# The middle steps' second product on GpSimd in four groups of six, and its two additions joined into one

## Chip, cores and metric

The kernel runs on one core of one Trainium2 chip. The metric is the device time of one execution in microseconds (us). Five engines work side by side: TensorE (PE in the profile, with its weight loads as PEld), VectorE (DVE), ScalarE (ACT), GpSimd (POOL) and SyncE (SP), which here only issues DMAs.

## What is computed

Two blocks follow each other, all in float32. The first mixes a sequence in the frequency domain: a real FFT over 3008 tokens, a product with a complex filter, and the inverse FFT, for 8 images with 256 channels. The second is a gated feed-forward block over the 24064 resulting tokens.

```python
X = np.fft.rfft(x, axis=1)                    # x: 8 x 3008 x 256
y = np.fft.irfft(X * (filt_r + 1j * filt_i)[None], n=3008, axis=1)
x = y.reshape(8 * 3008, 256)
g = x @ w_gate                                # 256 x 1536
silu = g * (1.0 / (1.0 + np.exp(-g)))
out = (silu * (x @ w_val)) @ w_out            # 1536 x 256
```

## The kernel before

**Tiling.** The FFT is done as small matrix products, in three stages: along one factor of the length, then with the twiddle factors and the filter (the middle steps), then back. The feed-forward block takes an image in 4 chunks (k), and each chunk in 3 groups (g) of the hidden width, so an image has 12 groups, numbered 0 to 11 (`step = 3 * k + g` from the second image on). A group multiplies sums of activations by sums of weights (tokens P, Q, A, B, E with their pairs), which saves products at the price of additions: those fall to VectorE, ScalarE and GpSimd.

**The order of the work** is written out by hand. `SCHEDULE` (line 87) is one list of tokens for a whole group; a loop over it (line 1384) issues each token's instructions, and every engine works through its own in that order (`pin`, which keeps program order). A token with a quote mark belongs to the group before. Tokens that matter here:

- `P Q A B E`: products on TensorE (line 1036), into banks `wk`, `wa`, `we`
- `x s y e`: what is put into a bank before a product is added to it; `e13` is such an operation on VectorE (line 333, output `we`), `y` the same into SBUF
- `m l g u h v`: copies and activations on ScalarE (lines 1071, 1078), subtractions and products on VectorE (lines 329, 1083)
- `D`: differences on GpSimd (line 329, `D<-f,f`); `S`: the sums of products that the output projection needs, on GpSimd too (lines 326 and 329, `h<-h`); `S00'` and `S01'` come first, near the start of the next group
- `n1 n2 n3`: the next chunk's sums (`combine_sequence`, GpSimd and ScalarE, output `y_t`). They are issued only where the group is the last of its chunk (`sequence_of`, line 1287), that is in groups 2, 5, 8 and 11
- `W`, `o`, `z`, `x.o`: output projection, its additions on VectorE, a transposition on VectorE, and the output DMAs on SP's queue
- `b0` to `b7`: one more piece of the next image's FFT at each of them (line 1399)

**The middle steps.** While images 1 to 6 are in the feed-forward block, the next image is prepared in these pieces. `fours(w)` (line 739) is one middle step, a generator that stops at each `yield` and goes on at the next `b` token; w = 0 to 6 runs in groups 4 to 10 (line 1346). For w below 6 it does, in turn: the products of the first stage's values (line 761, bank `wqb`); copies of these to SBUF on ScalarE (`raw`, line 775); the product with the real part of the filter on VectorE (line 779, into y); at `b4` the DMAs that bring `raw`, with real and imaginary rows swapped, into a tile q (line 596, `lent<-raw`); at `b5` and `b6` the product of q with the other part of the filter, half of the tile each (line 818); at `b7` the additions y = y + q on GpSimd (line 326, `lent<-lent`, 128x512), and the DMA that loads the next step's filter (`load_filter`, line 727, `lent<-filter`) into the same buffer. The next step's products read y at its `b0` (line 749).

x, y, q, filter and the tables of these steps all lie in one SBUF tile, `lent`, by which name the profile knows them. Reloads of the group's weights (`wt_t<-w_all`, line 477) go through SP's queue as well, at the tokens Q2, A12, A23 and B03, each when the matmuls that read the old weights are done.

Of the kernel before, what the change touches and what calls it, by code (L numbers as in the profile page):

```python
# [44 lines left out]
ALU = mybir.AluOpType  # L45
# [158 lines left out]
def kernel(  # L204
# [10 lines left out]
    nc = tc.nc  # L215
# [43 lines left out]
    def room_of(tag, u=0):  # L259

        first, units, count = fours[tag]
        a = (first + u % count * units) * NV * C
        return lent[:, a:a + units * NV * C]
# [31 lines left out]
    pin = tc.keep_in_program_order  # L295
# [29 lines left out]
    def add(eng, dst, a, b):  # L325
        return eng.tensor_tensor(out=dst, in0=a, in1=b, op=ALU.add)  # L326

    def sub(eng, dst, a, b):
        return eng.tensor_tensor(out=dst, in0=a, in1=b, op=ALU.subtract)  # L329
# [239 lines left out]
    def bank(name):  # L569
        return wps.tile([128, 512], FP32, name=f"w{name}", tag="w")  # L570
# [10 lines left out]
    class Spectral:  # L581
# [157 lines left out]
        def fours(self, w):  # L739

            tb = self.tb.pop(w)
            home, there = [], []
            if w:
                home = [bank(f"qc_{self.b}_{w}_{e}") for e in range(2)]
                y = self.p.pop(w - 1)
                for s in (0, 2, 1, 3):
                    for e in range(2):
                        r = slice(64 * e, 64 * e + 64)
                        pin(nc.tensor.matmul(  # L749
                            out=home[e][s // 2 * 64:s // 2 * 64 + 64, s % 2 * C:s % 2 * C + C],  # L750
                            lhsT=tb[r, 1, 64 * s:64 * s + 64], rhs=y[r, s],
                            start=s % 2 == 0, stop=True, skip_group_check=True))
            if w < N_FOUR:
                t = self.t2.pop(w)
                there = [bank(f"qb_{self.b}_{w}_{p}") for p in range(2)]
                for s in range(2):
                    for e in range(2):
                        for p in range(2):
                            r = slice(64 * p, 64 * p + 64)
                            a = 64 * (2 * s + e)  # L760
                            pin(nc.tensor.matmul(  # L761
                                out=there[p][64 * e:64 * e + 64, ts(s, C)],
                                lhsT=tb[r, 0, a:a + 64], rhs=t[r, s, e],
                                start=s == 0, stop=True, skip_group_check=True))
            yield
            z = y = None
            raw = []
            if w < N_FOUR:
                y = self.p[w] = room_of("y").rearrange("p (s c) -> p s c", c=C)
                there = [t.rearrange("p (s c) -> p s c", c=C) for t in there]  # L770

            def keep(p):
                t = t1pool.tile([128, NV, C], FP32, name=f"raw_{self.b}_{w}_{p}", tag="t1", bufs=2)
                raw.append(t)
                pin(nc.scalar.copy(out=t, in_=there[p]))

            def real(p):
                a = slice(2 * p, 2 * p + 2)
                pin(nc.vector.tensor_tensor(out=y[:, a], in0=there[p], in1=self.f[w][:, 0, a],
                                            op=ALU.mult))  # L780

            if home:
                z = room_of("g").rearrange("p (h f) -> p h f", h=2)
                pin(nc.scalar.copy(out=z[:, 0], in_=home[0]))
                pin(sub(nc.vector, z[:, 1], z[:, 0], home[1]))
            if there:
                keep(0)
            yield
            if home:
                pin(add(nc.vector, z[:, 0], z[:, 0], home[1]))  # L790
            if there:
                keep(1)
                real(0)
            yield
            if there:
                real(1)
            if home:
                rows = self.d2_tokens.rearrange("(h n) (r s) c -> (n r) h (s c)", h=2, r=2)
                for p in range(2):
                    at = (4 * w - 4 + 2 * p) * C  # L800
                    pin(nc.scalar.dma_start(out=rows[:, :, at:at + 2 * C],
                                            in_=z[64 * p:64 * p + 64]))
            yield
            q = None
            if there:
                q = room_of("e").rearrange("p (s c) -> p s c", c=C)
                for p in range(2):
                    pairs = [t.rearrange("(q r) s c -> q r s c", r=2)
                             for t in (q[:, 2 * p:2 * p + 2], raw[p])]
                    for r in range(2):  # L810
                        self.load(out=pairs[0][:, r], in_=pairs[1][:, 1 - r])
                self.load_four(w + 1)
            self.load_turns(w + 1)
            yield
            for half in range(2):
                a = slice(2 * half, 2 * half + 2)
                if there:
                    pin(nc.vector.tensor_tensor(out=q[:, a], in0=q[:, a], in1=self.f[w][:, 1, a],  # L818
                                                op=ALU.mult))
                yield  # L820
            for half in range(2 if there else 0):
                a = slice(2 * half, 2 * half + 2)
                pin(add(nc.gpsimd, y[:, a], y[:, a], q[:, a]))
            if there:
                self.f.pop(w)
            self.load_filter(w + 1)

# [503 lines left out]
    for b in range(B):  # L1331
# [35 lines left out]
        for step in range(NCHUNK * NG + (b == B - 1)):  # L1367
# [16 lines left out]
            for place, token in enumerate(SCHEDULE):  # L1384
# [4 lines left out]
                op = token.rstrip("'")  # L1389
# [76 lines left out]
```

## Time and profile before

| | us |
|---|---|
| three timed runs | 2838.08, 2839.66, 2836.62 |
| median | 2838.08 |
| the profiled run | 2833.91 |
| its span, first to last instruction | 2832.1 |

| what | count | mean ns | busy us |
|---|---|---|---|
| line 818, VectorE, 128x512 (the second product) | 72 | 959 | 69.1 |
| line 779, VectorE, 128x512 (the first product) | 72 | 682 | 49.1 |
| line 326, GpSimd, `lent<-lent` 128x512 | 84 | 1271 | 106.8 |
| line 326, GpSimd, `h<-h` 128x376 | 190 | 986 | 183.4 |
| line 329, GpSimd, `h<-h` 128x376 | 572 | 999 | 558.7 |
| line 333, VectorE, `we<-wk,c` 128x376 | 96 | 547 | 52.6 |
| line 1036, TensorE, 188 columns, `wa` | 4464 | 323 | 879.2 |

72 of the 84 in the third row are the additions of the middle steps; the other 12 belong to the second image's preparation. The granted clock of TensorE is 0.998 of its full speed, and one group lasts about 28.5 us.

How such rows are read: a group's row gives its line, engine and operation, what it writes and reads by the program's names, the shape, how often it ran, the busy time and the mean. A timeline's row starts with the start in us from the span's beginning and the duration; "x4" says how many instructions are merged; in brackets stands how long the engine was idle before, and what ended that. Matmuls overlap, and a duration of 0.80 for four of them is longer than their spacing.

### The profile page before, as it was taken

The page shows a single profiled execution, that of the slowest core. Times are in us where ns is not written, and L with a number is a line of the kernel's source. Part 1 is how long each engine was busy: PE and PEld are TensorE (multiplying, and loading weights), DVE is VectorE, ACT ScalarE, POOL GpSimd, SP SyncE. Part 2 cuts the span into 40 slices and gives each one's busy share as a digit, 9 for nine tenths or more (in the row PEclk, how much of TensorE's full clock was granted, in tenths as well). Part 3 has the DMA queues.
Part 4 walks back from the last instruction along what each step waited for, and adds up shares of the span by engine and source line. Part 5 has one row for each costly group of instructions (what it writes and reads, how often), then busy time and mean ns, then how long its engine had stood idle before and what let it go on. Part 6 is the DMA issues. An engine that isn't in the chain of part 4 may idle for free.

```text
span 2832.1 us, 48560 instructions
## 1 busy us (share of the span) xinstructions
PE 2784.2 (98%) x15432; PEld 2312.1 (82%) x15432; DVE 2033.8 (72%) x4603; ACT 1565.8 (55%) x4202; POOL 1524.9 (54%) x1671
## 2 busy tenths in 40 slices
PE   7999999999999999999999999999999999999998
PEld 5777878888888888788888888888888888888887
DVE  6898766777667767677766677667776767766666
ACT  6775445555555555555555555555554555555554
POOL 4886576464545554446554455444555454545543
PEclk9999999999999999999999999999999999999999
DMA  9687866877666775767666676667766777655543
GB/s 231 216 274 251 270 209 217 291 234 229 180 187 205 246 225 168 204 217 226 218 183 201 213 240 201 186 191 234 227 203 179 215 222 224 194 147 153 152 137 82
DMA packets 363373, 586.59 MB, mean 207 GB/s; under 512 B 198388, under 2 KB 246260, under 8 KB 363024
## 3 DMA queue, kind: packets, MB, share of 16 engines
q1 hardware_dynamic: 337922, 534.73, 60.8%
q10 hardware_dynamic: 23406, 45.43, 5.9%
q0 software_dynamic: 1792, 3.34, 0.5%
q8 instruction: 125, 2.05, 0.3%
q14 instruction: 128, 1.05, 0.1%
HBM read 467.87 MB, written 101.34 MB: 201 GB/s over the span
## 4 chain that ended last, share of the span: by engine, by line
PE 85%; DVE 4%; POOL 3%; issue 2%; DMA 1%; ACT 0%; SPq 0%; POOLq 0%; DVEq 0%
PE wa L1036 23%; PE wk L1036 16%; PE wA L1133 16%; PE we L1036 12%; PE wG L1133 8%; PE wF L1133 4%; PE pd L939 3%; PE wqa L690 2%; PE wqc L749 1%; PE wqb L761 1%; POOL out_dram L1118 1%; POOL h L329 1%; DVE lent L818 1%; DVE y L333 1%; DVE o L326 0%
## 5 line engine op out<-in xcount | busy, mean ns | idle before, releaser
L1036 PE MATMUL wa<-y_t,wt_t 128*128 128x188 f32 x4464 | 879.2, 323 | 6.8 <-DMA y_t<-yt 2.0
L1036 PEld LDWEIGHTS wa<-y_t,wt_t 128*128 128x128 f32 x4464 | 745.6, 190 | 84.8 <-ACT wa L1062 11.1
L1036 PEld LDWEIGHTS wk<-y,wt_t 128*128 128x128 f32 x2976 | 494.7, 190 | 106.1 <-issue 33.4
L1036 PE MATMUL wk<-y,wt_t 128*128 128x188 f32 x2976 | 571.2, 325 | 0.0
L329 POOL TENSOR_TENSOR h<-h 128x376 f32<-128x376 f32 x572 | 558.7, 999 | 15.4 <-DVE h L326 15.2
L326 POOL TENSOR_TENSOR h<-h 128x376 f32<-128x376 f32 x190 | 183.4, 986 | 702.5 <-DVE h L1083 702.5
L1133 PE MATMUL wA<-h,wo_t 128*128 128x376 f32 x1532 | 551.1, 482 | 3.6 <-DVE o L326 3.5
L1036 PE MATMUL we<-y_t,wt_t 128*128 128x188 f32 x2232 | 433.6, 323 | 5.1 <-DVE we L333 4.2
L329 POOL TENSOR_TENSOR D<-f,f 128x376 f32<-128x376 f32 x288 | 279.6, 985 | 253.9 <-ACT f L1051 253.8
L329 DVE TENSOR_TENSOR we<-we,m 128x376 f32<-128x376 f32 x576 | 318.5, 554 | 120.0 <-PE we L1036 62.4
L1036 PEld LDWEIGHTS we<-y_t,wt_t 128*128 128x128 f32 x2232 | 368.2, 190 | 10.4 <-DVE we L333 8.2
L1133 PEld LDWEIGHTS wA<-h,wo_t 128*128 128x128 f32 x1532 | 274.9, 190 | 113.7 <-issue 10.7
L1071 ACT COPY m<-wa 128x376 f32<-128x376 f32 x576 | 273.0, 474 | 86.7 <-PE wa L1036 83.4
L333 DVE SCALAR_TENSOR_TENSOR y<-wk,c 128x376 f32<-128x376 f32 x480 | 246.4, 539 | 57.7 <-ACT c L1055 35.3
L1078 ACT ACTIVATE g<-wa 128x188 f32<-128x188 f32 x576 | 187.8, 326 | 163.9 <-PE wa L1036 153.3
L1078 ACT ACTIVATE u<-we 128x188 f32<-128x188 f32 x576 | 188.5, 328 | 155.3 <-DVE we L329 148.9
L1133 PE MATMUL wG<-h,wo_t 128*128 128x376 f32 x768 | 274.0, 479 | 0.0
L1055 ACT COPY c<-wk 128x376 f32<-128x376 f32 x288 | 136.3, 473 | 221.2 <-PE wk L1036 194.2
L1051 ACT ACTIVATE f<-wk 128x376 f32<-128x376 f32 x288 | 140.4, 487 | 169.3 <-PE wk L1036 133.1
L1067 ACT COPY we<-y 128x376 f32<-128x376 f32 x480 | 221.8, 481 | 18.8 <-DVE h L1083 14.5
L1083 DVE TENSOR_TENSOR h<-wa,g 128x188 f32<-128x188 f32 x576 | 198.4, 345 | 33.0 <-ACT g L1078 32.8
L1083 DVE TENSOR_TENSOR h<-we,u 128x188 f32<-128x188 f32 x576 | 197.4, 343 | 27.0 <-ACT u L1078 16.0
(162 smaller groups left out, 3512.9 us busy)
## 6 DMA issues: line engine op xcount, KB each, us to landing
wt_t<-w_all SPq DMA_DIRECT2D x174, 896.0 KB, 4.8
wt_t<-w_all SPq DMA_DIRECT2D x174, 768.0 KB, 4.5
lent<-filter SPq DMA_DIRECT2D x36, 1024.0 KB, 6.9
lent<-d SPq DMA_DIRECT2D x84, 256.0 KB, 4.6
d<-lent ACTq DMA_DIRECT2D x84, 256.0 KB, 3.8
d<-lent ACTq DMA_DIRECT2D x96, 192.0 KB, 3.3
lent<-raw SPq DMA_DIRECT2D x144, 128.0 KB, 2.8
t<-d SPq DMA_DIRECT2D x112, 128.0 KB, 4.5
```

Source lines behind the costliest of these rows:

```text
L326: return eng.tensor_tensor(out=dst, in0=a, in1=b, op=ALU.add)
L329: return eng.tensor_tensor(out=dst, in0=a, in1=b, op=ALU.subtract)
L333: return nc.vector.scalar_tensor_tensor(out=dst, in0=a, scalar=-1.0, in1=b, op0=ALU.mult, op1=ALU.subtract)
L939: pin(nc.tensor.matmul(out=rows, lhsT=self.t4[k, i][:, j, ts(cb, 128)], rhs=cols, start=j == 0, stop=True, skip_group_check=True))
L1036: pin(nc.tensor.matmul(out=ps[:, z], lhsT=self.wt[:, SLOT[p], z], rhs=rhs, start=start and z == 0, stop=True, skip_group_check=True))
L1051: pin(act.mul(self.small(f"f{i}", f"f{i}", 1), t[f"k{i}"], -1.0))
L1055: pin(act.copy(out=self.small(f"c{i}", f"c{i}", 1), in_=t[f"k{i}"]))
L1067: pin(act.copy(out=self.bank(f"e{at}"), in_=t[f"y{at}"]))
L1071: pin(act.copy(out=self.small(f"m{at}", "m", 4), in_=t[f"a{at}"]))
L1078: pin(act.activation(out=self.small(op, "g", 3, 1)[:, 0], in_=ps[:, 1], func=AF.Silu))
L1083: pin(v.tensor_tensor(out=dst, in0=ps[:, 0], in1=g, op=ALU.mult))
L1133: pin(nc.tensor.matmul(out=self.tiles[at], lhsT=wo_t[:, JB * q + i, WO[p], :], rhs=self.hs[i][:, HID[p]], start=start and i == 0, stop=Tru ...
```

## The change

In the middle steps, the second product of w = 0, 2, 3 and 5 is issued on GpSimd; w = 1 and 4 stay on VectorE. For all w the two additions of half a tile become one of the whole tile (128x1024), issued once both halves of the product are made. The tokens at which all of these are issued stay the same.

```diff
             for half in range(2):
                 a = slice(2 * half, 2 * half + 2)
                 if there:
-                    pin(nc.vector.tensor_tensor(out=q[:, a], in0=q[:, a], in1=self.f[w][:, 1, a],
-                                                op=ALU.mult))
+                    e = nc.vector if w % 3 == 1 else nc.gpsimd
+                    pin(e.tensor_tensor(out=q[:, a], in0=q[:, a], in1=self.f[w][:, 1, a],
+                                        op=ALU.mult))
                 yield
-            for half in range(2 if there else 0):
-                a = slice(2 * half, 2 * half + 2)
-                pin(add(nc.gpsimd, y[:, a], y[:, a], q[:, a]))
             if there:
+                pin(add(nc.gpsimd, y, y, q))
                 self.f.pop(w)
             self.load_filter(w + 1)
```

## Prediction

> **What bounds the kernel now.** I began with the page's table of engines:
>
> ```profile
> PE 2784.2 (98%) x15432; PEld 2312.1 (82%) x15432; DVE 2033.8 (72%) x4603; ACT 1565.8 (55%) x4202; POOL 1524.9 (54%) x1671
> ```
>
> TensorE is busy for 98% of the span, so an edit on VectorE or GpSimd can only win back moments in which TensorE stands still. The second view is the list of waits, for TensorE alone, between 560 and 2450 us, where all the middle steps lie. It has one line:
>
> ```profile
> PE we L1036 <- DVE we L333: 4.2, 12, 0.3
> ```
>
> Twelve waits, always for the operation of line 333 that fills a bank `we` before products are added to it. Six images are prepared in this stretch, so that is two waits an image. To place them I went to the timeline of one group with such a wait (627 to 645 us, image 2's preparation, w = 2), first on VectorE and TensorE:
>
> ```profile
> 636.33 0.34 DVE L1083 TENSOR_TENSOR h<-wk,g 128x188 f32<-128x188 f32 x1
> 636.59 1.07 DVE L818 TENSOR_TENSOR lent<-lent 128x512 f32<-128x512 f32 x1
> 637.58 0.34 DVE L1083 TENSOR_TENSOR h<-wa,g 128x188 f32<-128x188 f32 x1
> 637.85 0.53 DVE L333 SCALAR_TENSOR_TENSOR y<-wk,c 128x376 f32<-128x376 f32 x1
> 638.30 1.31 DVE L818 TENSOR_TENSOR lent<-lent 128x512 f32<-128x512 f32 x1
> 639.53 0.54 DVE L333 SCALAR_TENSOR_TENSOR y<-wk,c 128x376 f32<-128x376 f32 x1
> ...
> 641.06 0.53 DVE L329 TENSOR_TENSOR we<-we,m 128x376 f32<-128x376 f32 x1
> 641.49 0.55 DVE L333 SCALAR_TENSOR_TENSOR we<-wk,c 128x376 f32<-128x376 f32 x1
> ...
> 640.93 0.82 PE L1036 MATMUL wa<-y_t,wt_t 128*128 128x188 f32 x4
> 642.09 0.90 PE L1036 MATMUL we<-y_t,wt_t 128*128 128x188 f32 x4 [0.34 <-DVE we L333]
> ```
>
> Read: VectorE runs without a break from 636.33 to 642; the two operations of line 818 are in that row; the product E13 (the `we` at 642.09) waits for e13 (the line 333 at 641.49). Such a block of four matmuls normally follows the last one after 0.64 us (the two `wa` blocks at 582.26 and 582.90 us, for example). Here it came after 1.16: 0.52 us lost. The view of waits counts 0.34 because it subtracts a modelled end. Measured start to start over all matmuls of the stretch, the twelve losses sum to 6.1 us, and w = 1 of the last prepared image (2321.25 us) loses another 0.23. The other gaps there are shorter than 0.12 us and stand at the same places in groups that have no line 818.
>
> **Why line 818 is dear in those groups.** It lasts 0.68 us in some places and 1.07 or 1.31 in others. The difference is GpSimd:
>
> ```profile
> 635.15 1.96 POOL L329 TENSOR_TENSOR h<-h 128x376 f32<-128x376 f32 x2
> 637.79 1.27 POOL L326 TENSOR_TENSOR lent<-lent 128x512 f32<-128x512 f32 x1 [0.68 <-PE wa L1036]
> 639.74 1.27 POOL L326 TENSOR_TENSOR lent<-lent 128x512 f32<-128x512 f32 x1 [0.68 <-DVE lent L818]
> ```
>
> The first half at 636.59 overlaps the subtraction that ends at 637.11, the second at 638.30 overlaps the addition of the first half. Of the 72, the 36 that touch no GpSimd operation average 0.680 us, the 36 that do 1.238.
>
> **What the Trainium skill says.** (1) "GPSIMD Engine Reference", section Key points: GpSimd shares its SBUF interfaces with VectorE, and VectorE instructions with two SBUF inputs contend. The trace agrees exactly: line 818 is the only VectorE group of the stretch whose two inputs both lie in SBUF, and the only one that lengthens. y of line 333 (one input in PSUM) takes 0.538 us under GpSimd and 0.539 clear of it, h of line 1083 0.346 and 0.345. (2) The same page, section Elementwise — side-by-side cycle accounting, gives 4497 ns on GpSimd against 2293 on VectorE for a two-input addition, and puts it down to the reading of two operands, not the arithmetic. The trace agrees in size: 1.271 us (addition, 128x512) against 0.680 is 1.87 times.
>
> **The change, part by part.** The steps of w = 0 to 5 fall into groups 4 to 9 of an image; w % 3 = 1 are groups 5 and 8, the last of a chunk, where GpSimd also forms the next sums. So w = 0, 2, 3, 5 move: 4 x 6 images x 2 halves = 48 of 72 multiplications.
>
> *VectorE* loses 48 slots. For w = 2 and 5 the slot is 0.99 + 1.23 us (636.59 to 637.58, 638.30 to 639.53), so 2.2 us in front of e13. What else could hold e13? It stands behind l12 (line 329), whose matmul E12 begins at 639.02 and is read from 639.82 on. Then e13 starts at about 640.25 and ends at 640.8; E13's regular place is 640.93 + 0.64 = 641.57. Margin 0.77 us: the 0.51 vanishes whole. Gain 6.1 us. For w = 0 and 3 the slots are 4 x 0.60 us an image, but no matmul waits in those groups: worth nothing.
>
> *GpSimd* gains 48 multiplications, which no row shows. Lower bound: a read of 512 elements at VectorE's speed, 0.68; upper: twice the addition, 2.5, since the arithmetic isn't what the page names as the limit. I take the addition's 1.27. From the rows of 376, 512 and 564 elements (0.985, 1.271, 1.383) an element costs 2.1 ns, so one addition of 1024 is an estimated 2.36 us instead of 2 x 1.27. Per group: 2 x 1.27 + 2.36 = 4.9 us. In w = 2 GpSimd comes free at 637.11 and ends at 642.0 (with 2.5: 644.5); its next work, the first sum of products of the group's S step, starts at 649.54, when VectorE's h is ready. 7.5 us are left (5.1). The result is read by the next group's products, later still. Cost nothing, hidden by GpSimd's idle time at each group's end (702.5 us in the row of that subtraction's idle time). The swapped halves arrive 3.2 us after their DMA issue (last issue of w = 2 at 628.0), before GpSimd comes free; where they come later (w = 3: 662.4 + 3.2 = 665.6, GpSimd free at 663.6) nothing stands behind the wait.
>
> *Slowing others.* The moved operations contend only with VectorE's two-SBUF-input ones, of which none is left in these groups. 0.
>
> *SP.* The next filter's load may start once the second multiplication has read the buffer: for w = 2 639.61 so far, now 637.11 + 2.54 = 639.65. Next in SP's queue is a reload of weights at 643.66, waiting for TensorE. 0 at 1.27, and 0 up to 3.0 us a multiplication.
>
> *w = 1 and 4* keep VectorE, but the joined addition now waits for both halves, so the second half no longer overlaps the first addition: 1.31 becomes 0.68, and with it goes the stray 0.23 (there the half lasted 1.60). GpSimd's addition ends at 610.91 + 2.36 = 613.3 instead of 612.9, and the sums behind it (612.90, 0.98 us, then 1.57 idle until ScalarE) shift by 0.4 within that idle time: 0. Fewer additions, 72 to 36: 0 off the path.
>
> *Sum:* -6.1 - 0.23 = -6.3 us on a span of 2832.1, hence 2825.8. That profiled run took 2833.91 us; the three timed ones 2836.62 to 2839.66. Applied to their median: 2838.08 - 6.3 = **2831.7**. Timed runs could have more strays of w = 1 and 4: twelve times 0.23 would be 2.8 more, 2829.
>
> **Rivals.**
> *A. As summed*, 2831.7, own range 2828.5 to 2833.
> *B. Part of the stall comes back.* E13 is released, and a ScalarE copy in the same row becomes the next limit. For: ScalarE's g at 640.10 sat 2.26 us behind y. Against: that y itself is delayed by line 818 and moves ahead with it; s23, the next one that a matmul needs, has about 0.8 us by the same count. Half the gain: 2835.
> *C. Nothing comes of it*, because e13 was held by l12's inputs and not by VectorE's row. Against: w = 0, 1 and 3 run the same tokens with no stall. 2838.
> *D. Slower: the multiplication on GpSimd is far dearer than its addition.* Place: w = 2 and 5, ahead of the next group's S step. GpSimd has 649.54 - 637.11 = 12.4 us for 2m + 2.36, so it decides from m = 5.0 us; beyond, each us of m delays twelve groups by 2 us. At m = 5.6: 12 x 1.2 = 14 us, less 6.3: 2846. For: no row shows m. Against: four times the addition.
> That the change does not do what it says is excluded by the group numbers above.
>
> **How the numbers follow.** A 0.66, B 0.14, C 0.12, D 0.08. A measurement can tell about 0.2% (5.7 us, 2832.4) from no change. A is faster by 0.22%, just beyond it, and I count 0.06 of it as falling within; B and C are within; D is slower. Range: down to A's strays, up to no change, which leaves out D and half of C above and little below: 2828.5 to 2838.1.
>
> **What would show it.** Right: no TensorE wait for line 333 in 560 to 2450 us; GpSimd multiplications near 1.27 us; joined additions near 2.36; the remaining 24 on VectorE all at 0.68. Wrong: GpSimd's first S subtraction of a group begins late after VectorE's h; a new wait of TensorE on ScalarE behind E13; SP's weight reload issued late.

## The result, and the profile after

The change makes the kernel faster by more than was predicted: 2827.52 us against 2837.22 for the kernel before, medians of six runs each; the ratio is 0.9965, with a 95% interval from 0.9953 to 0.9978. Forecast were 2831.7, and at least 2828.5. The profiled run of the changed kernel has a span of 2824.2 us.

The page's table of engines, after:

```profile
PE 2781.0 (98%) x15432; PEld 2314.5 (82%) x15432; DVE 1991.2 (71%) x4555; ACT 1572.9 (56%) x4202; POOL 1577.9 (56%) x1683
```

VectorE lost 42.6 us of busy time and GpSimd gained 53; neither figure says what the span does. The groups of instructions, with shapes kept apart, show what was built (busy us, mean ns; then idle time before):

```profile
L326 POOL TENSOR_TENSOR lent<-lent 128x1024 f32<-128x1024 f32 x36 | 85.0, 2362 | 42.1 <-PE wA L1132 40.2
L819 POOL TENSOR_TENSOR lent<-lent 128x512 f32<-128x512 f32 x48 | 60.4, 1283 | 1.2 <-PE pd L938 1.1
...
L819 DVE TENSOR_TENSOR lent<-lent 128x512 f32<-128x512 f32 x24 | 16.4, 682 | 0.0
```

The multiplication costs on GpSimd what the addition did, the joined addition costs 2.36 us, and the 24 that stay on VectorE are all at 0.68. The list of TensorE's waits between 560 and 2450 us, which had the one line for `we`, is empty. The timeline at the same place of the schedule as before (w = 2, image 2's preparation), VectorE first, then GpSimd and TensorE:

```profile
637.03 0.34 DVE L1082 TENSOR_TENSOR h<-wk,g 128x188 f32<-128x188 f32 x1
637.29 0.34 DVE L1082 TENSOR_TENSOR h<-wa,g 128x188 f32<-128x188 f32 x1
637.55 1.00 DVE L333 SCALAR_TENSOR_TENSOR y<-wk,c 128x376 f32<-128x376 f32 x2
639.28 0.55 DVE L326 TENSOR_TENSOR o<-o,wA 128x376 f32<-128x376 f32 x1 [0.73 <-PE wA L1132]
...
641.09 0.55 DVE L333 SCALAR_TENSOR_TENSOR we<-wk,c 128x376 f32<-128x376 f32 x1
...
637.76 2.52 POOL L819 TENSOR_TENSOR lent<-lent 128x512 f32<-128x512 f32 x2
640.36 2.37 POOL L326 TENSOR_TENSOR lent<-lent 128x1024 f32<-128x1024 f32 x1
649.61 1.92 POOL L326 TENSOR_TENSOR h<-h 128x376 f32<-128x376 f32 x2 [6.88 <-DVE h L1082]
...
641.62 0.80 PE L1035 MATMUL wa<-y_t,wt_t 128*128 128x188 f32 x4
642.26 0.80 PE L1035 MATMUL we<-y_t,wt_t 128*128 128x188 f32 x4
```

VectorE now has pauses, E13 follows its predecessor after the regular 0.64 us, and GpSimd still waits 6.88 us for the next group's first sum.

**Where the time came from.** The trace gives the start of every matmul. From the first matmul of W2 in a group to that of the next is one group's length. For one undisturbed image (image 2), in us, with the groups that the change shortened:

| kernel | w = 1 | w = 2 | w = 3 | w = 4 | w = 5 | whole image |
|---|---|---|---|---|---|---|
| before | 27.685 | 28.279 | 30.842 | 27.687 | 28.287 | 341.46 |
| after | 27.609 | 27.612 | 30.816 | 27.612 | 27.610 | 339.93 |
| gain | 0.08 | 0.67 | 0.03 | 0.08 | 0.68 | 1.53 |

w = 0 and 6, and the five other groups, are equal to 0.01 us. Over the images that prepare another one (1 to 6) the lengths fall from 2045.05 to 2036.05 us, 9.0; one of these images has an unrelated 0.21 in the changed kernel, without which it is about 9.2.

The spans differ by only 7.9. The rest stands where no edited line runs: image 0 takes 377.2 us in the first profile of the kernel before and 378.7 after, while the head and the tail of the span together are 0.4 shorter after. A second look at the kernel before (last experiment) gives 379.7 for image 0. So the first profile was a short draw, and the timed difference of 9.7 us belongs beside the 9.2, not beside 7.9; the interval of the ratio reaches from 6 to 13 us.

### The profile page after: what moved, and what is told of

It is laid out like the page before. It is cut to its first block, busy times and chain, and to the rows that moved or that the text cites. A ratio compares the mean times of both kernels' runs of the same rounds, so it can differ in the third digit from the quotient of the medians.

```text
span 2824.2 us, 48474 instructions
## 1 busy us (share of the span) xinstructions
PE 2781.0 (98%) x15432; PEld 2314.5 (82%) x15432; DVE 1991.2 (71%) x4555; ACT 1572.9 (56%) x4202; POOL 1577.9 (56%) x1683
## 3 DMA queue, kind: packets, MB, share of 16 engines
q14 instruction: 128, 1.05, 0.1%
## 4 chain that ended last, share of the span: by engine, by line
PE 82%; POOL 1%; issue 1%; DVE 0%; DMA 0%; ACT 0%; POOLq 0%; ACTq 0%; DVEq 0%
PE wa L1035 22%; PE wk L1035 15%; PE wA L1132 15%; PE we L1035 11%; PE wG L1132 7%; PE wF L1132 4%; PE pd L938 3%; PE wqa L690 1%; PE wqc L749 1%; PE wqb L761 1%; POOL out_dram L1117 0%; POOL h L329 0%; DMA out_dram<-o 0%; DVE o L326 0%; DVE h L329 0%
```

## Experiments

The diffs are against the changed kernel, unless they say otherwise. Each result's interval is that of the ratio to the kernel before, measured in the same series. Lengths of an image are read from W2 to W2 as above, on images 2 to 5, leaving out those in which a group without an edited line is 0.1 to 0.5 us longer in that run alone.

### Joined additions alone

```diff
-                    e = nc.vector if w % 3 == 1 else nc.gpsimd
+                    e = nc.vector
```

> All multiplications stay on VectorE; only the two additions become one. Theory 1 (contention): E13 is late because the halves of line 818 are stretched by GpSimd; without an addition between the halves the second one takes 0.68 us instead of 1.31, e13 comes 0.6 us sooner, and the stall in w = 2 and 5 is gone (regular groups of 27.6 us, an image 339.9 to 340.2 us from step to step against 341.43 before). Gain 7.5 to 9 us, as large as that of the whole change. Theory 2 (occupancy): any line 818 on VectorE in those groups is too much; w = 2 and 5 keep a stall of at least 0.3 us, an image stays at 340.7 or more, and the gain is below 5 us.

Measured: 2827.47 us against 2836.52, ratio 0.9968 [0.9956, 0.9980]; an image 339.94 to 339.97 us, w = 2 at 27.63. This is the whole gain, with not one operation moved to GpSimd. All instructions of line 819 in this kernel (min/median/max in ns), and then w = 2's timeline on VectorE and GpSimd:

```profile
L819 DVE TENSOR_TENSOR lent<-lent x72: 674/680/1093, 582.6 to 2428.0; 128x512 f32<-128x512 f32 x72
```

```profile
639.98 1.09 DVE L819 TENSOR_TENSOR lent<-lent 128x512 f32<-128x512 f32 x1
640.99 0.34 DVE L1082 TENSOR_TENSOR h<-wa,g 128x188 f32<-128x188 f32 x1
641.26 0.53 DVE L333 SCALAR_TENSOR_TENSOR y<-wk,c 128x376 f32<-128x376 f32 x1
641.71 0.68 DVE L819 TENSOR_TENSOR lent<-lent 128x512 f32<-128x512 f32 x1
...
638.56 1.96 POOL L329 TENSOR_TENSOR h<-h 128x376 f32<-128x376 f32 x2
642.52 2.37 POOL L326 TENSOR_TENSOR lent<-lent 128x1024 f32<-128x1024 f32 x1 [2.00 <-PE wA L1132]
```

The first half still meets the subtraction that ends at 640.52 and takes 1.09. The second has GpSimd to itself and takes 0.68, where it took 1.31. These 0.63 us are enough: e13 comes in time, and TensorE has no wait for line 333 between 560 and 2450 us. Theory 2 falls.

### Moved multiplications alone

```diff
             if there:
-                pin(add(nc.gpsimd, y, y, q))
+                for half in range(2):
+                    a = slice(2 * half, 2 * half + 2)
+                    pin(add(nc.gpsimd, y[:, a], y[:, a], q[:, a]))
                 self.f.pop(w)
```

> Multiplications of w = 0, 2, 3, 5 on GpSimd, the additions still two. Both theories: the stall in w = 2 and 5 is gone with its 0.10 us of restart (12 x 0.62 = 7.4 us), since no line 818 is left on VectorE there. w = 1 and 4 keep the second half stretched to 1.31 us and with it 0.05 us of stall each, and the 0.02 us ahead of W1 in five groups stays if it comes from the second addition's wait: an image of 340.1 to 340.2 us against 339.94 of the change. Gain 7 to 8 us.

Measured: 2829.53 us, ratio 0.9977 [0.9968, 0.9986]; an image 340.14 to 340.16 us, w = 1 and 4 at 27.68, w = 2 and 5 at 27.63. As expected in each part: the stall is gone this way too, the 0.05 us of w = 1 and 4 stay, and so do 0.024 us ahead of W1 in five groups an image. The timed difference to the joined additions alone is 2 us, and the two intervals overlap; the 0.2 us an image is read from the traces.

### All multiplications on GpSimd

```diff
-                    e = nc.vector if w % 3 == 1 else nc.gpsimd
+                    e = nc.gpsimd
```

> All multiplications on GpSimd, w = 1 and 4 too, additions joined. If GpSimd has room there (its row was idle for 2.0 and 0.7 us before the two additions, and the multiplications can start when its S work ends, at about 607.7 us of 612.9), w = 1 and 4 stay at 27.61 us and an image at 339.9: the same as the change within 1 us. If the sums behind are pushed back, the first sums of products (S00) come late in the groups after them, W1 waits for them, and the groups after w = 1 and 4 lengthen by up to 1 us each: up to 12 us slower than the change.

Measured: 2825.47 us, ratio 0.9969 [0.9956, 0.9981]; an image 339.93 us, w = 1 and 4 at 27.61. GpSimd has the room, and keeping w = 1 and 4 off it wasn't needed. In time the two kernels can't be told apart.

### The changed kernel again

> The changed kernel once more, beside the other three on the same chip, so that they can be set against it: 9 to 10 us below the kernel before, an image of 339.94 us in the trace.

Measured: 2828.10 us, ratio 0.9973 [0.9962, 0.9984]; an image 339.93 us.

### The overlap put back

Against the joined additions alone:

```diff
             if there:
+                pin(add(nc.gpsimd, raw[0], y[:, 0:2], q[:, 0:2]))
                 pin(add(nc.gpsimd, y, y, q))
```

> As the kernel with joined additions alone (all multiplications on VectorE), plus one addition on GpSimd of the first half of y and q into a tile that nobody reads: it waits for the first multiplication only, as the old first addition did, so GpSimd works again beside the second half of line 818. Extra work in all 36 middle steps; the output is unchanged. Contention: the second half goes back to 1.31 us in w = 1, 2, 4 and 5, the stall of 0.51 us with its restart of 0.1 returns in w = 2 and 5, and 0.05 in w = 1 and 4: an image at 341.2 to 341.4 us, no gain over the kernel before. If the joined addition helped in another way (one wait fewer for the readers of y, a different order of signals), y still has one writer here, and the image stays at 339.9 to 340.0.

Measured: 2834.91 us against 2836.53, ratio 0.9994 [0.9985, 1.0002]; an image 341.10 us, w = 2 and 5 at 28.19. TensorE's waits from 560 to 2450 us, and all instructions of line 819:

```profile
PE we L1036 <- DVE we L333: 3.8, 12, 0.3
```

```profile
L819 DVE TENSOR_TENSOR lent<-lent x72: 680/870/1503, 582.0 to 2433.8; 128x512 f32<-128x512 f32 x72
```

An addition whose result nobody reads brings back the twelve waits, at the same place. So it is the overlap that made the stall, and not the count of writers of y. Missed was w = 1 and 4: they stay at 27.61, and with them the image is 0.1 shorter than expected. The useless addition starts a little earlier than the old first one did, so that the second half meets 0.71 us of it instead of 0.76, and takes 1.26 us, not 1.32; that e13 came just in time for this reason is read from the timelines. The 0.05 us before would then be an edge. The 0.024 us ahead of W1 stay away as well, so they don't come from the overlap.

### How much room GpSimd has

```diff
+                    for _ in range(4 if w % 3 != 1 else 0):
+                        pin(e.tensor_tensor(out=raw[half], in0=q[:, a], in1=self.f[w][:, 1, a],
+                                            op=ALU.mult))
                     pin(e.tensor_tensor(out=q[:, a], in0=q[:, a], in1=self.f[w][:, 1, a],
                                         op=ALU.mult))
```

> The changed kernel with four more multiplications of the same operands, into a tile that nobody reads, ahead of each half on GpSimd in w = 0, 2, 3, 5: a multiplication that costs 5 x 1.27 = 6.4 us. The rival of the prediction that ends slower, with its own formula: GpSimd has 12.4 us for 2m + 2.4 in w = 2 and 5, so beyond m = 5.0 each group loses 2 x (6.4 - 5.0) = 2.7 us, 12 groups make 33 us, w = 0 and 3 (15 us of room or more) a little. If the late first sums of products are only needed by W1 and by the differences that stand behind them, some 3.5 us after they start, the loss stays below 1.5 us a group, under 18 us in all.

Measured: 2852.98 us, ratio 1.0055 [1.0039, 1.0070], 24.9 above the 2828.10 of the changed kernel. That is between the two expectations, and neither names the right reader:

```profile
PE wqc L749 <- POOL lent L326: 19.9, 14, 1.6
```

TensorE waits for the joined addition itself. The next step's first products read y at the head of the next group, before W1 needs anything of the S step. The groups after w = 2 and 5 lengthen by 1.67 us each, 20 us in all; three groups after w = 3 lose 0.5 to 1.3 more. In the kernel before, these products start at 651.81 us, 14.7 after GpSimd comes free, where the prediction counted 12.4 up to the S step. By its own formula the multiplication would begin to cost at an estimated (14.7 - 2.4) / 2, about 6 us, instead of 5.0. The price of a slow multiplication was real; its place was put one consumer too late.

### Both result banks freed at once

```diff
                 pin(nc.scalar.copy(out=z[:, 0], in_=home[0]))
-                pin(sub(nc.vector, z[:, 1], z[:, 0], home[1]))
+                pin(nc.vector.tensor_copy(out=z[:, 1], in_=home[1]))
+                pin(sub(nc.vector, z[:, 1], z[:, 0], z[:, 1]))
...
-                pin(add(nc.vector, z[:, 0], z[:, 0], home[1]))
+                pin(nc.vector.scalar_tensor_tensor(out=z[:, 0], in0=z[:, 0], scalar=2.0,
+                                                   in1=z[:, 1], op0=ALU.mult,
+                                                   op1=ALU.subtract))
```

> The changed kernel, and at the start of a middle step both result banks of the step before are copied out at once, one by ScalarE, one by VectorE, and difference and sum are formed from the copies (sum as twice the first less the difference). Reading of the trace to be tested: W1, in groups 5 to 10 of an image, waits for the second of these banks until VectorE's addition has read it, and loses 0.05 us and 0.07 of restart. With the bank free 1.3 us sooner these go: groups w = 1 to 6 shorter by 0.05 to 0.13 us each, an image at 339.2 to 339.6 us, 2 to 4.6 us below the changed kernel. If W1 waits for something else (sums of products from GpSimd, ScalarE's copies), or if the extra 0.6 us on VectorE delays the first product of the middle step, the groups keep 27.61 us or grow.

Measured: 2826.95 us, ratio 0.9967 [0.9954, 0.9979]; an image 339.85 us. w = 1 to 5 came down by 0.13 us each, to 27.48 and 30.69, but w = 6 went up by 0.55. VectorE's timeline at w = 1 and at w = 6, and GpSimd beside the latter:

```profile
601.42 0.69 DVE L791 SCALAR_TENSOR_TENSOR lent<-lent 128x512 f32<-128x512 f32 x1
...
1081.86 1.40 DVE L791 SCALAR_TENSOR_TENSOR lent<-lent 128x512 f32<-128x512 f32 x1
1083.19 0.53 DVE L1060 SCALAR_TENSOR_TENSOR x<-wk,f 128x376 f32<-128x376 f32 x1
...
1081.74 0.98 POOL L329 TENSOR_TENSOR D<-f,f 128x376 f32<-128x376 f32 x1 [0.96 <-ACT f L1053]
1082.68 2.37 POOL L329 TENSOR_TENSOR h<-h 128x376 f32<-128x376 f32 x2
```

The 0.13 us are what stood at W1: its first matmul came 0.21 us after the one before it and its second 0.391 after the first, and here both follow at their regular spacing, 0.159 and 0.316. That is what was expected if W1 waits for this bank. The new operation reads two SBUF tiles. In w = 1 to 5 it runs while GpSimd pauses; in w = 6, which has fewer matmuls ahead of it, it falls onto `D` and `S`, and takes 1.40 us instead of 0.69. VectorE's next operation starts 0.94 us later against the matmuls than in the changed kernel; 0.71 of that is this contention, the rest the added copy. GpSimd's pair of subtractions takes 2.37 us there, 1.92 at this place in the changed kernel: both sides pay.

### The same, except in w = 6

```diff
-                pin(nc.vector.tensor_copy(out=z[:, 1], in_=home[1]))
-                pin(sub(nc.vector, z[:, 1], z[:, 0], z[:, 1]))
+                if there:
+                    pin(nc.vector.tensor_copy(out=z[:, 1], in_=home[1]))
+                pin(sub(nc.vector, z[:, 1], z[:, 0], z[:, 1] if there else home[1]))
...
```

The sum is chosen by `there` in the same way. The diff is against the kernel with both banks freed in all steps.

> The changed kernel with the two copies of the result banks in w = 1 to 5 only; w = 6 keeps difference and sum from the bank. With the copies in all, w = 6 lost 0.55 us (the sum from two SBUF tiles took 1.40 us beside GpSimd's work, 0.69 elsewhere) and the other five gained 0.13 each. Without the loss an image comes to 339.94 - 5 x 0.13 = 339.3 us, 6 images to 3.9 us below the changed kernel: about 2823.7 us beside a kernel before of 2836.5, ratio 0.9955. If the loss of w = 6 was not the contention but the bank order, w = 1 to 5 or the groups behind w = 6 show a new wait and the image stays near 339.8.

Measured: 2823.80 us against 2836.26, ratio 0.9957 [0.9943, 0.9970]; an image 339.29 us, w = 6 back at 26.618. Since the whole edit is left out of w = 6, this run does not part the contention there from the added copy. This is the fastest kernel of the study. Its interval overlaps that of the changed kernel; that it is faster by 6 x 0.65 = 3.9 us rests on the matmul starts, where every image shows it.

### The kernel before, a second trace

> The kernel before once more, for its trace. The first profile of it (2832.1 us, from a run of 2833.9) lies below all its timed runs (2836.5 to 2839.7), and its first image takes 377.2 us where every changed kernel's takes 378.5 to 379.7, though no edited line runs there. If that profile was a lucky draw, this one shows 378.5 us or more for the first image, 341.4 for each of the others and a span near 2835. If the change slows the first image, it is 377.2 again.

Measured: 2839.40 us, span 2837.6, image 0 379.7 us, images 2 to 5 341.42 to 341.48; image 1 has 3.9 us more in a group that no edit touches. The profile is a sample: two images at the start vary by some us from run to run, most of the rest repeats to 0.05 us.

## Why the prediction was right, and where it failed

**Right.** The place: twelve stalls of TensorE at E13, two an image, behind line 818, in w = 2 and 5. They are gone, and nothing took their place; ScalarE's s23 had room, as B's counter-argument said. The prices on GpSimd (1.27 forecast, 1.28 measured; 2.36 and 2.36), the 0.68 of those left on VectorE, the cost of nothing for w = 0 and 3, on SP and for the sums of the next chunk. Without its stall, e13 ends 0.62 us before E13 starts (641.64 and 642.26); the prediction had worked out a margin of 0.77.

**Wrong, the term "6.1".** The sum took 0.51 us for each stall, start to start, and set every other gap under 0.12 us aside as standing in groups without line 818 too. Four terms were lost that way: the second to the fifth of this table. Set side by side, the two traces' matmul starts of one image give:

| term | us each | times | us |
|---|---|---|---|
| the stall itself | 0.51 | 12 | 6.1 |
| second matmul after it, 0.263 after the first instead of 0.159 | 0.10 | 12 | 1.2 |
| a matmul shortly ahead of it, 0.19 after its predecessor instead of 0.159 | 0.03 | 12 | 0.4 |
| e13 at the edge in w = 1 and 4 | 0.05 | 12 | 0.6 |
| W1, groups of w = 1 to 5 | 0.024 | 30 | 0.7 |
| the stray of w = 1 | 0.29 | 1 | 0.3 |

Together 9.3, against 9.2 from the group lengths and 9.7 timed. The forecast had 6.3. The largest mis-sized term is the stall with what belongs to it, forecast 6.1 and measured 7.7. The gaps at W1 do stand in groups without line 818, as the prediction said, but not all of their length does: they were 0.24 us start to start in groups w = 1 to 5 and 0.21 after; in the groups without line 818 that have this gap it is 0.22 in both kernels. The range's lower end was made from strays of w = 1 and 4 alone and missed the median by 1.0 us. The base added 0.9 us to the miss: the forecast set out from 2838.08, the median of three runs, where six give 2837.22. In gain, 6.3 us stood against 9.7.

**Wrong, the cause within the change.** The prediction gave the 6.1 to the move and 0.23 to the joined addition. The joined addition alone gives all of it, the move alone most of it, and together they give no more than the first: both undo the same stall. The prediction had both numbers on the page (the slot of 1.23 us would become 0.60, and e13 needed to come 0.51 us sooner), but subtracted the whole slot for the move and never asked what the other half of the edit did in w = 2 and 5. That the stall comes from the overlap is shown from both sides, by taking the overlapping addition away and by putting a useless one back. It agrees with the Trainium skill, "GPSIMD Engine Reference", section Key points: VectorE instructions with two SBUF inputs contend with GpSimd, with which VectorE shares its SBUF interfaces. These runs add the numbers: 0.68 us alone, mostly 1.25 to 1.32 under an addition, 1.60 in the stray of w = 1.

**Rivals.** B and C did not happen. D's mechanism is real beyond some size; its consumer was misread, as the sixth experiment shows. No multiplication here came near it. A slip of the prediction that changed nothing: the 702.5 us of idle time stand before an addition (line 326), not a subtraction.

**Open.** Why the joined addition shortens the wait ahead of W1 by 0.024 us: ScalarE's copy of the first bank starts 1.14 us after the matmuls' start instead of 1.17, and TensorE's first products have one wait for GpSimd fewer. Two writers of y bring the longer wait (moved multiplications alone), one writer with a useless addition does not (the overlap put back). But in w = 6 the copy starts after 1.14 us in the kernel before too, with two writers of y. So the missing wait alone does not explain it, and the cause stays open.

## What to carry to other kernels

Ask what an operation overlaps before asking which engine it should be on: of two VectorE instructions of one line that read two SBUF tiles, the one beside a GpSimd operation took up to 2.3 times as long here, and moving or merging the GpSimd work can be worth as much as moving the VectorE work. When an edit has two halves, make the sum for each half alone, too. When counting what a stall costs, take the matmuls behind it until they are back at their regular spacing, and compare small gaps by size, not only by place.

## Not expected of the hardware

- After a stall, the second matmul starts 0.263 us after the first where the regular spacing of 188 columns is 0.159: each stop costs 0.10 us more than the wait. For 376 columns it is 0.391 instead of 0.316.
- A half of line 818 that starts beside a GpSimd instruction is not slowed evenly. In the kernel before, all 36 of them end 0.55 us after the end of that instruction, whether 0.51 or 1.05 us of it were left: 637.66 after 637.11, 639.61 after 639.06. So of the 0.68 us that the work takes alone, 0.55 come after GpSimd is done, and the price is what is left of GpSimd's instruction less 0.13 us.
- Contention can cost GpSimd too, where it is the one that starts later (seen in w = 6 where both banks are freed at once). `D`, which had begun first, keeps its 0.98 us; VectorE's operation ends 0.55 us after it; and GpSimd's next subtraction, begun meanwhile, takes 1.43 us instead of 0.98.
- VectorE operations with one input in PSUM were not slowed at all: 0.54 us for line 333 with and without GpSimd at work.
